# A recurrent attention kernel on one core: the last segment and the drain written as loop passes instead of a tail of their own

## The chip, the cores and the metric

The kernel runs on one core of one Trainium2 chip. A core has a matrix engine (TensorE: PE for matmuls, PEld for its weight loads), VectorE (DVE), ScalarE (ACT), GpSimd (POOL) and a queue that issues transfers (SyncE, SP). The metric is device time in microseconds (us) of one execution. Before the change it is 822.81 us, the median of 3 runs (822.68 to 822.87).

## The reference

The input x has 2048 rows of 512. One branch is an attention over segments of 32 rows with a memory of 8 rows that goes from segment to segment; the other is a layer norm with a two-layer MLP; a gate g of each row mixes both.

```python
mem = mem0
for s in range(64):
    h = concat([mem, x[:, 32 * s:32 * s + 32]])        # 40 rows
    q, k, v = h @ Wq, h @ Wk, h @ Wv                   # 32 heads of 128
    p = softmax(mask(q @ k.T * scale))                 # 40 x 40 for each head
    o = (p @ v) @ Wo
    mem, out_s = o[:8], o[8:]
a = concat(out_0 .. out_63)
b = gelu(layernorm(x) @ w1 + b1) @ w2 + b2
out = g * a + (1 - g) * b
```

The memory that segment 63 leaves is read by nobody.

## The kernel before

The work has two stages. The first, to about 100 us, loads the weights and x and computes the MLP branch and the gates into `c_all` and `g_all`. The second is a loop over the 64 segments (L636), four to a tile of 128 rows; `T, si` are the tile and the segment's place in it. All matmuls of the loop use 32 columns of PE, four products side by side.

A segment handles 32 rows: 8 of memory and 24 of x. The other 8 x rows of each of a tile's four segments ("left" rows) are projected together, as side work of the segments of the tile before (`side_work`, L334). The side work of a tile's fourth segment is `out_units(T - 2)`, which selects the output rows of a tile, adds the MLP branch on DVE (L329) and stores them (L330), and `wo_left(T - 1)`, the output projection of the left rows. These are generators: `run_fill` puts a few of their matmuls where PE would wait. Their results stand in PSUM banks 5 and 6 in turn (`side`, L194); the copies out of them are queued in `dve_q` and `act_q` and are put into the program when `flush` is called.

In order, a segment's pass does this:

- `ux_out(s - 2)` (L630): four ACT copies of the x part of an earlier segment's product into `UTT`, one for each bank.
- `prep_h`, `prep_q`, `x_mul(s - 1)` (L615) on POOL: the x part of the probabilities, `Px`, for the segment before, and the running sum of reciprocals, `racc`.
- Q, K, V (L211, L222), DVE transposes (L217), copies, the scores (L383, L387) on top of a mask that `mask_mm` (L374) wrote into the bank beforehand, and two exponentials on ACT (L685, L686), whose sums go into `hist`.
- The memory half: sums (L688), reciprocal (L692), `Pm` in two parts (L695), the product with V (`av`, L398 and L403), four copies into `UTT` (L703), then the sums and the reciprocal of the x part (L699, L704).
- The output projection (`wo_unit`, L233): 32 matmuls of 512 columns for the memory rows of this segment and the x rows of the segment two before, then a copy to `wsb` (L711).
- The mask of the next segment, the product of `Px` of the segment before with V (`av_x`, L625), and the new memory (L365, L721).

A segment's x rows so reach the output projection two passes later. The pass of segment 63 breaks off after its scores (L683), and a tail of its own follows (L725 to L789): it leaves out the memory half of segment 63; it does the x half on DVE (L733 to L736) instead of POOL; it copies the U banks on DVE and ACT in turn (L755, L763, L765); it runs the projections of segments 61, 62 and 63 (`wo_x`, L744) and that of tile 15's left rows in two halves of 256 columns (L774); and it adds and stores tile 15 in two halves (L788, L789).

The program order of the loop and the tail is kept on each engine (`manual_schedule`, L599 to L790). What stands behind it is placed by the framework where an engine is free: the flag that tells whether any sum overflowed. `hist` is reduced and tested (L796, L799), `racc` likewise (L797, L800), a product with one element counts the partitions that passed (`cnt`, L801 and L802, in one of the two side banks), `bad` follows on DVE (L804), and every engine loads it (L805) and branches on it (L808), past a slow fallback for overflow.

Of the kernel before, what the change touches and what calls it, by code (L numbers as in the profile page):

```python
# [8 lines left out]
FP32 = mybir.dt.float32  # L9
BF16 = mybir.dt.bfloat16  # L10
# [13 lines left out]
def kernel(ctx, tc, A_x, A_mem0, A_Wq, A_Wk, A_Wv, A_Wo, A_seg_len, B_x, B_w1, B_b1, B_w2, B_b2, gate_w, out):  # L24
# [576 lines left out]
    prep_q(0)  # L601
    nc.gpsimd.memset(UTT[1][:, :, :, 0:40], 0.0)
    nc.gpsimd.memset(racc[:], 0.0)
    nc.gpsimd.memset(hist[:], 0.0)
    warm = cw.tile([P, 1], FP32, tag="warm", bufs=1, name="warm")
    nc.scalar.activation(out=warm[:], in_=g_all[:, 0:1], func=ACTF.Exp)
    S_next = mask_mm()
# [25 lines left out]
        for j, U in enumerate(Uxs.pop(s)):  # L633
            nc.scalar.copy(out=UTT[T % 2][:, :, j, c0 + M:c0 + 40], in_=U[:])  # L634

    for s in range(nseg):  # L636
        T, si = divmod(s, SPT)
        last = s == nseg - 1
        hc, hn = hT[s % NHT], hT[(s + 1) % NHT]
        fill = side_work(T, si)  # L640
        if si == 1 and T + 2 < NT:
            x_load(T + 2)
        if si == 3 and T + 1 < NT:
            left_v_in(T + 1)
        if si == 3 and T + 2 < NT:
            x_left(T + 2)
        B, S = S_next
        na, nb, nc_, nd, ne = ring
        ring = (nb, nd, ne, na, nc_)
        qk_banks = (na, nb, nc_, nd, ne)  # L650
        if s >= 2:
            ux_out(s - 2)
            flush(act_q)
        if s + 1 < nseg:
            prep_h(s + 1)
        if s >= 1:
            prep_q(s)
            x_mul(s - 1)
        flush(dve_q)
        BANKS = [(0,) + HF[0], (1,) + HF[0], (0,) + HF[1], (1, H // 2, 3 * H // 4), (1, 3 * H // 4, H)]  # L660
        for bi, (t, h0, h1) in enumerate(BANKS):
            bk = bank(qk_banks[bi], [P, 512])
            for kc in range(KC):
                qk_unit(bk, hc, t, h0, h1, kc)
            Tv = qk_tr(bk, h0, h1)
            dst = QT[:, h0:h1, 0:32] if t == 0 else KT[:, h0:h1, :]
            (nc.gpsimd.tensor_copy if bi == 2 else nc.scalar.copy)(out=dst, in_=Tv)  # L667
        V = cw.tile([P, NG, Dh], BF16, tag="V", name="V")
        Vs[s] = V
        vb0, vb1 = bank(na, [P, 512]), bank(nb, [P, 512])  # L670
        for kc in range(KC):
            v_unit(vb0, hc, 0, kc)
        nc.scalar.copy(out=v_out(V, 0), in_=vb0[:])
        flush(dve_q, 9)
        scores(S, s, 0, 3 * NG // 4)
        v_unit(vb1, hc, 1, 0)
        scores(S, s, 3 * NG // 4, NG)
        for kc in range(1, KC):
            v_unit(vb1, hc, 1, kc)
        E = cw.tile([P, NG, EW], BF16, tag="E", name="E")  # L680
        R = cw.tile([P, NG * 40], FP32, tag="R", name="R")
        Es[s], Rs[s] = E, R
        if last:  # L683
            break
        nc.scalar.activation(out=E[:, :, 0:16], in_=S[:, :, 0:16], func=ACTF.Exp, scale=scale, accum_out=hist[:, s, 0:1])  # L685
        nc.scalar.activation(out=E[:, :, 16:EW], in_=S[:, :, 16:EW], func=ACTF.Exp, scale=scale, accum_out=hist[:, s, 1:2])  # L686
        sm = bank(nc_, [P, NG, 8])
        sums(sm, E[:, :, 8:16], True, False)  # L688
        sums(sm, E[:, :, 0:8], False, True)
        nc.scalar.copy(out=v_out(V, 1), in_=vb1[:])  # L690
        run_fill(5 + (si == 3))
        nc.vector.reciprocal(out=R[:, 0:8 * NG].rearrange("p (i q) -> p i q", q=8), in_=sm[:])  # L692
        Pm = cw.tile([P, NG, 16], BF16, tag="Pm", bufs=1, name="Pm")
        for c in (8, 0):
            nc.vector.tensor_tensor(out=Pm[:, :, c:c + 8], in0=E[:, :, c:c + 8], in1=R[:, 0:8 * NG].rearrange("p (i q) -> p i q", q=8), op=ALU.mult)  # L695
        Um = [bank(k, [P, NG, 8]) for k in (nd, ne, na, nc_)]
        av(Um, 8, s, V, Pm, 8, 0, 0)
        sr = B[:, 0:NG * 32].rearrange("p (i q) -> p i q", q=32)
        sums(sr, E[:, :, 16:48], True, False)  # L699
        sums(sr[:, :, 24:32], E[:, :, 48:56], False, True)  # L700
        Tp, sp = divmod(s - 2, SPT)
        for j in range(4):
            (nc.scalar.copy if j % 2 else nc.vector.tensor_copy)(out=UTT[Tp % 2][:, :, j, 24 - 8 * sp:24 - 8 * sp + M], in_=Um[j][:])  # L703
        nc.vector.reciprocal(out=R[:, 8 * NG:].rearrange("p (i q) -> p i q", q=32), in_=sr)  # L704
        run_fill(1)
        flush(act_q, 2)
        wsb = cw.tile([P, Dm], BF16, tag="wsb", bufs=9, name="wsb")
        wp = bank(nb, [P, Dm])
        for u in range(8):
            wo_unit(wp, UTT[Tp % 2], 24 - 8 * sp, u)  # L710
        nc.scalar.copy(out=wsb[:], in_=wp[:])  # L711
        if s >= 2:
            wsbs[s] = wsb
        S_next = mask_mm()
        if s >= 1:
            av_x(s - 1, (nd, ne, na, nc_))
        run_fill(2 * (si == 3))
        if s + 1 < nseg:
            aT = S_next[0][:, NG * EW:NG * EW + KC * M].rearrange("p (k m) -> p k m", m=M)
            mem_out(aT, wsb)  # L720
            nc.vector.tensor_copy(out=hn[:, :, 0:M], in_=aT)  # L721
        for _ in fill:
            pass

    nc.scalar.activation(out=E[:, :, 16:EW], in_=S[:, :, 16:EW], func=ACTF.Exp, scale=scale, accum_out=hist[:, s, 1:2])  # L725
    nc.scalar.copy(out=v_out(V, 1), in_=vb1[:])
    av_x(s - 1, (nd, ne, na, nc_))
    sr = B[:, 0:NG * 32].rearrange("p (i q) -> p i q", q=32)
    sums(sr, E[:, :, 16:48], True, False)
    sums(sr[:, :, 24:32], E[:, :, 48:56], False, True)  # L730
    Rl = R[:, 8 * NG:]
    Rq = Rl.rearrange("p (i q) -> p i q", q=32)
    nc.vector.reciprocal(out=Rq, in_=sr)  # L733
    Px = cw.tile([P, NG, 40], BF16, tag="Px", name="Px")
    nc.vector.tensor_tensor(out=Px[:, :, 0:32], in0=E[:, :, 16:48], in1=Rq, op=ALU.mult)
    nc.vector.tensor_tensor(out=Px[:, :, 32:40], in0=E[:, :, 48:56], in1=Rq[:, :, 24:32], op=ALU.mult)  # L736
    nc.gpsimd.tensor_tensor(out=racc[:, 8 * NG:], in0=racc[:, 8 * NG:], in1=Rl, op=ALU.add)
    Es.pop(s), Rs.pop(s)
    Pxs[s] = Px
    for _ in fill:  # L740
        pass
    flush(act_q, 9)

    def wo_x(sw, k, ut, c0):  # L744
        wp = bank(k, [P, Dm])
        for u in range(8):
            wo_unit(wp, ut, c0, u)
        wsb = cw.tile([P, Dm], BF16, tag="wsb", bufs=9, name="wsb")
        nc.scalar.copy(out=wsb[:], in_=wp[:])
        wsbs[sw + 2] = wsb  # L750

    U1, U0 = UTT[(NT - 1) % 2], UTT[NT % 2]
    wo_x(s - 2, nb, U1, 16)
    for j, U in enumerate(Uxs.pop(s - 1)):
        (nc.vector.tensor_copy if j % 2 else nc.scalar.copy)(out=U1[:, :, j, 8 + M:48], in_=U[:])  # L755
    for _ in out_units(NT - 2):
        flush(dve_q, 9)
    av_x(s, (nd, ne, na, nc_))
    wo_x(s - 1, nb, U1, 8)

    Ul = Uxs.pop(s)
    for j, U in enumerate(Ul):
        (nc.vector.tensor_copy if j % 2 else nc.scalar.copy)(out=U0[:, :, j, M:32], in_=U[:, :, 0:RIDE])  # L763
    for j, U in enumerate(Ul):
        (nc.vector.tensor_copy if j % 2 else nc.scalar.copy)(out=U1[:, :, j, 32:40], in_=U[:, :, RIDE:32])  # L765
    wo_x(s, 6, U0, 0)
    T = NT - 1
    HD2 = Dm // 2
    wL = cw.tile([P, Dm], BF16, tag="wsbL", bufs=1, name="wsbL")
    for half in range(2):  # L770
        d = slice(HD2 * half, HD2 * half + HD2)
        wp = bank((nc_, nd)[half], [P, HD2])
        for u in range(8):
            wo_unit(wp, U1, 32, u, HD2 * half, HD2 * half + HD2)  # L774
        (nc.vector.tensor_copy if half else nc.scalar.copy)(out=wL[:, d], in_=wp[:])
    o_sb = cw.tile([P, Dm], BF16, tag="o", bufs=1, name="o")
    obs = [bank(k, [P, HD2]) for k in (ne, nb)]
    for half in range(2):
        d = slice(HD2 * half, HD2 * half + HD2)
        for si in range(SPT):  # L780
            nc.tensor.matmul(obs[half][32 * si:32 * si + 32, :], lhsT=SelX[:], rhs=wsbs[SPT * T + si + 2][:, d], start=True, stop=False,
                             tile_position=(0, 32 * si))
    for half in range(2):
        d = slice(HD2 * half, HD2 * half + HD2)
        for si in range(SPT):
            nc.tensor.matmul(obs[half][32 * si:32 * si + 32, :], lhsT=SelL[si][:], rhs=wL[:, d], start=False, stop=True,
                             tile_position=(0, 32 * si))
        nc.vector.scalar_tensor_tensor(out=o_sb[:, d], in0=obs[half][:], scalar=g_all[:, T:T + 1], in1=c_all[:, T, d], op0=ALU.mult, op1=ALU.add)  # L788
        nc.sync.dma_start(out2[T * P:(T + 1) * P, d], o_sb[:, d])  # L789
    man.__exit__(None, None, None)  # L790


# [130 lines left out]
```

## Time and profile before

| | us |
|---|---|
| median of 3 runs | 822.81 (822.68 to 822.87) |
| the profiled execution | 822.87 |
| its span, first to last instruction | 821.1 |
| PE busy | 793.0 (97%) |
| DVE, ACT, POOL busy | 493.1, 446.6, 272.7 |
| granted TensorE clock, mean | 0.998 |

From the trace's table of stretches, with what PE was busy in each:

| stretch, us from the start | length | PE busy |
|---|---|---|
| 785.77 to 796.54 (segment 62) | 10.77 | 9.35 |
| 796.54 to 806.78 (segment 63 and side work) | 10.24 | 10.17 |
| 806.78 to 816.75 (rest of the tail) | 9.97 | 7.12 |
| 816.75 to 821.10 (store, branch, end) | 4.35 | 0.00 |

A line of the timeline has the start, the duration, the engine, the source line, the operation, its tiles and shapes, and in brackets how long the engine idled before and who ended that. A line of the chain has the start, the duration, the engine and the source line of one link of the work that ended last. A line on one source line of the kernel has the engine, the operation, how often it ran, its shortest, median and longest duration in ns, and its first and last start.

### The profile page before, as it was taken

The page shows a single profiled execution, that of the slowest core. Times are in us where ns is not written, and L with a number is a line of the kernel's source. Part 1 is how long each engine was busy: PE and PEld are TensorE (multiplying, and loading weights), DVE is VectorE, ACT ScalarE, POOL GpSimd, SP SyncE. Part 2 cuts the span into 40 slices and gives each one's busy share as a digit, 9 for nine tenths or more (in the row PEclk, how much of TensorE's full clock was granted, in tenths as well). Part 3 has the DMA queues.
Part 4 walks back from the last instruction along what each step waited for, and adds up shares of the span by engine and source line. Part 5 has one row for each costly group of instructions (what it writes and reads, how often), then busy time and mean ns, then how long its engine had stood idle before and what let it go on. Part 6 is the DMA issues. An engine that isn't in the chain of part 4 may idle for free.

```text
span 821.1 us, 48437 instructions
## 1 busy us (share of the span) xinstructions
PE 793.0 (97%) x22013; PEld 443.4 (54%) x22013; DVE 493.1 (60%) x1022; ACT 446.6 (54%) x1239; POOL 272.7 (33%) x624
## 2 busy tenths in 40 slices
PE   6999999999999999999999999999999999999986
PEld 3666545555555555555555555555555555555543
DVE  5764256565656666665666565666566565756554
ACT  3555445655555555555555645555565555565553
POOL 8100224242434243243424242423333242424220
PEclk9999999999999999999999999999999999999999
DMA  9791310000000010101010100101010101010000
GB/s 314 238 404 48 104 28 11 25 16 15 25 20 26 10 36 10 37 11 33 6 38 10 31 17 20 27 18 28 10 36 11 36 4 40 7 34 8 10 5 24
DMA packets 38357, 37.59 MB, mean 46 GB/s; under 512 B 13561, under 2 KB 36578, under 8 KB 36610
## 3 DMA queue, kind: packets, MB, share of 16 engines
q1 hardware_dynamic: 38018, 34.31, 12.6%
q8 instruction: 174, 2.85, 1.5%
q14 instruction: 37, 0.30, 0.1%
q0 software_dynamic: 128, 0.13, 0.1%
HBM read 26.03 MB, written 6.29 MB: 39 GB/s over the span
## 4 chain that ended last, share of the span: by engine, by line
PE 92%; DVE 4%; issue 1%; DMA 1%; SPq 1%; ACT 1%; DVEq 0%; ACTq 0%
PE b L211 33%; PE b L233 18%; PE b L222 16%; PE b L398 5%; PE hp L470 4%; PE bp L487 4%; PE b L360 3%; PE b L374 2%; PE b L365 2%; PE b L383 2%; PE b L403 1%; DVE R L692 1%; DMA Wo_sb<-in_A_x_dram 1%; DVE Pm L695 1%; PE b L387 0%
## 5 line engine op out<-in xcount | busy, mean ns | idle before, releaser
L217 DVE STREAM_TRANSPOSE Tt<-b 128x512 f32<-128x512 f32 (+1 forms) x384 | 225.6, 613 | 82.2 <-PE b L211 70.3
L211 PEld LDWEIGHTS <-hT 128*32 128x32 bf16 x5120 | 131.3, 97 | 108.2 <-DVE hT L721 23.5
L233 PE MATMUL b<-Wo_sb,UTT 128*32 128x512 bf16 (+1 forms) x2656 | 160.9, 378 | 1.3 <-ACT UTT L763 0.9
L222 PE MATMUL b<-Wv_sb,hT 128*32 128x512 bf16 x2048 | 141.8, 378 | 0.0
L211 PE MATMUL b<-Wq_sb,hT 128*32 128x512 bf16 x2048 | 133.3, 380 | 3.2 <-DVE hT L721 1.7
L211 PE MATMUL b<-Wk_sb,hT 128*32 128x256 bf16 (+1 forms) x3072 | 133.3, 308 | 0.0
L667 ACT CAST KT<-Tt 128x256 bf16<-128x256 f32 (+1 forms) x192 | 87.1, 476 | 53.6 <-DVE Tt L217 53.5
L620 POOL TENSOR_TENSOR Px<-E,R 128x256 bf16<-128x256 bf16 x63 | 42.5, 675 | 208.9 <-DVE R L704 208.9
L704 DVE RECIPROCAL R<-b 128x256 f32<-128x256 f32 x63 | 110.7, 1757 | 0.0
L667 POOL CAST QT<-Tt 128x512 bf16<-128x512 f32 x64 | 39.2, 613 | 187.1 <-DVE Tt L217 187.1
L233 PEld LDWEIGHTS <-UTT 128*32 128x32 bf16 x2656 | 64.4, 96 | 63.8 <-DVE UTT L703 12.2
L711 ACT CAST wsb<-b 128x512 bf16<-128x512 f32 x63 | 36.9, 586 | 111.2 <-PE b L233 111.2
L692 DVE RECIPROCAL R<-b 128x64 f32<-128x64 f32 x63 | 35.1, 557 | 78.4 <-PE b L360 78.4
L634 ACT CAST UTT<-b 128x256 bf16<-128x256 f32 x248 | 74.4, 386 | 9.7 <-PE b L403 7.5
L667 ACT CAST QT<-Tt 128x512 bf16<-128x512 f32 x64 | 39.6, 619 | 68.7 <-DVE Tt L217 68.7
L222 PEld LDWEIGHTS <-hT 128*32 128x32 bf16 x2048 | 49.4, 96 | 21.2
L475 ACT ACTIVATE hg<-hp,b_sb 128x256 bf16<-128x256 f32 x80 | 37.8, 474 | 39.9 <-PE hp L470 39.9
L721 DVE CAST hT<-b 128x32 bf16<-128x32 f32 x63 | 12.1, 191 | 79.0 <-PE b L365 79.0
L398 PEld LDWEIGHTS <-V 32*128 32x128 bf16 x4064 | 34.4, 91 | 45.6 <-DVE Pm L695 32.3
L470 PE MATMUL hp<-yT,w_sb 128*128 128x256 bf16 (+1 forms) x352 | 54.7, 281 | 2.2 <-DMA w_sb<-in_B_w_dram 0.9
L703 ACT CAST UTT<-b 128x64 bf16<-128x64 f32 x126 | 20.6, 215 | 66.1 <-PE b L403 66.1
L622 POOL TENSOR_TENSOR racc<-racc,R 128x320 f32<-128x320 f32 x63 | 54.9, 871 | 0.0
(131 smaller groups left out, 1056.5 us busy)
## 6 DMA issues: line engine op xcount, KB each, us to landing
Wv_sb<-in_A_Wv_dram SPq DMA_DIRECT2D x4, 1024.0 KB
Wq_sb<-in_A_Wq_dram SPq DMA_DIRECT2D x4, 1024.0 KB
Wk_sb<-in_A_Wk_dram SPq DMA_DIRECT2D x4, 1024.0 KB
Wo_sb<-in_A_Wo_dram SPq DMA_DIRECT2D x2, 2048.0 KB
vd<-vt SPq DMA_DIRECT2D x32, 128.0 KB
vs<-vd SPq DMA_DIRECT2D x256, 16.0 KB
out_dram<-o SPq DMA_DIRECT2D x15, 128.0 KB
Wo_sb<-in_A_x_dram SPq DMA_DIRECT2D x1, 1024.0 KB
```

What stands on the lines that cost most here:

```text
L211: nc.tensor.matmul(bk[32 * j:32 * j + 32, 0:n], lhsT=G[:, kc, :], rhs=W5[t][:, kc, h0:h1, j, :], start=(kc == 0), stop=(kc == KC - 1), til ...
L217: nc.vector.transpose(out=Tt[:, 0:n], in_=bk[:, 0:n])
L222: nc.tensor.matmul(bk[32 * j:32 * j + 32, :], lhsT=G[:, kc, :], rhs=Wv5[:, kc, 4 * vb:4 * vb + 4, j, :], start=(kc == 0), stop=(kc == KC - ...
L233: nc.tensor.matmul(bk[32 * g:32 * g + 32, :], lhsT=ut[:, i, j, c0:c0 + 32], rhs=Wo_sb[:, 4 * i + j, d0:d1], start=(j == 0 and i < 4), stop ...
L398: nc.tensor.matmul(U[j][:, i, :], lhsT=V[q, i, :], rhs=Pt[q, i, c_main:c_main + n], start=(i == 0), stop=False, skip_group_check=True, til ...
L470: nc.tensor.matmul(hp[:rows, :], lhsT=w1_sb[:, kc, fc * P:fc * P + rows], rhs=yTs[blk][:, kc, :], start=(kc == 0), stop=(kc == KC - 1))
L620: nc.gpsimd.tensor_tensor(out=Px[:, :, 0:32], in0=E[:, :, 16:48], in1=Rr, op=ALU.mult)
L622: nc.gpsimd.tensor_tensor(out=racc[:], in0=racc[:], in1=R[:], op=ALU.add)
L634: nc.scalar.copy(out=UTT[T % 2][:, :, j, c0 + M:c0 + 40], in_=U[:])
L667: (nc.gpsimd.tensor_copy if bi == 2 else nc.scalar.copy)(out=dst, in_=Tv)
L692: nc.vector.reciprocal(out=R[:, 0:8 * NG].rearrange("p (i q) -> p i q", q=8), in_=sm[:])
L704: nc.vector.reciprocal(out=R[:, 8 * NG:].rearrange("p (i q) -> p i q", q=32), in_=sr)
```

## The change

The tail of its own goes. The loop runs over `nseg + 2` passes. Pass 63 is a full pass, with the memory half, whose result is not read. Passes 64 and 65 only drain: `ux_out`, `x_mul` and `av_x` for what is left, and a whole projection each. The rest of tile 14 and tile 15 follow behind the loop with the same generators that the loop uses, each in one piece of 512 columns. The memset of `hist` (L604) goes too, since all of `hist` is now written. The matmuls' tiling, the sums, `Pm` and everything in passes 0 to 62 stay as they are (much of the diff is indentation).

```diff
-    nc.gpsimd.memset(hist[:], 0.0)
...
-    for s in range(nseg):
+    for s in range(nseg + 2):
         T, si = divmod(s, SPT)
-        last = s == nseg - 1
+        live = s < nseg
         hc, hn = hT[s % NHT], hT[(s + 1) % NHT]
-        fill = side_work(T, si)
+        if live:
+            fill = side_work(T, si)
...
-        if last:
-            break
...
+        else:
+            if s == nseg:
+                ux_out(s - 2)
+                x_mul(s - 1)
+                av_x(s - 1, (nd, ne, na, nc_))
+            else:
+                ux_out(s - 2)
+            flush(dve_q)
+            Tp, sp = divmod(s - 2, SPT)
         wsb = cw.tile([P, Dm], BF16, tag="wsb", bufs=9, name="wsb")
         wp = bank(nb, [P, Dm])
         for u in range(8):
...
-        S_next = mask_mm()
-        if s >= 1:
+        if s + 1 < nseg:
+            S_next = mask_mm()
+        if live and s >= 1:
             av_x(s - 1, (nd, ne, na, nc_))
...
-    nc.scalar.activation(out=E[:, :, 16:EW], in_=S[:, :, 16:EW], func=ACTF.Exp, scale=scale, accum_out=hist[:, s, 1:2])
...
-    nc.vector.reciprocal(out=Rq, in_=sr)
...
-    wo_x(s - 2, nb, U1, 16)
-    for j, U in enumerate(Uxs.pop(s - 1)):
-        (nc.vector.tensor_copy if j % 2 else nc.scalar.copy)(out=U1[:, :, j, 8 + M:48], in_=U[:])
-    for _ in out_units(NT - 2):
-        flush(dve_q, 9)
-    av_x(s, (nd, ne, na, nc_))
-    wo_x(s - 1, nb, U1, 8)
...
-    wo_x(s, 6, U0, 0)
...
-            wo_unit(wp, U1, 32, u, HD2 * half, HD2 * half + HD2)
...
-        nc.vector.scalar_tensor_tensor(out=o_sb[:, d], in0=obs[half][:], scalar=g_all[:, T:T + 1], in1=c_all[:, T, d], op0=ALU.mult, op1=ALU.add)
-        nc.sync.dma_start(out2[T * P:(T + 1) * P, d], o_sb[:, d])
+    flush(act_q, 9)
+    for _ in out_units(NT - 2):
+        flush(dve_q, 9)
+    for _ in wo_left(NT - 1):
+        pass
+    flush(act_q, 9)
+    for _ in out_units(NT - 1):
+        pass
+    flush(dve_q, 9)
     man.__exit__(None, None, None)
```

## The prediction

> **What bounds the kernel now.** I read the page's first and fourth parts first: TensorE (PE) is busy 97% of the span and holds 92% of the chain that ended last.
>
> ```profile
> span 821.1 us, 48437 instructions
> PE 793.0 (97%) x22013; PEld 443.4 (54%) x22013; DVE 493.1 (60%) x1022; ACT 446.6 (54%) x1239; POOL 272.7 (33%) x624
> PE 92%; DVE 4%; issue 1%; DMA 1%; SPq 1%; ACT 1%; DVEq 0%; ACTq 0%
> ```
>
> Then I read the diff against the rows. Column tiles of 32, the sums, Pm in two parts (L695 runs twice in each segment) and the projection with 512 columns are all in the trace of before. The loop for segments 0 to 62 is the same text, indented. What differs is the end: segment 63 and all behind it. So the question is the last 25 us, and there PE waits for others. The timeline of before's end:
>
> ```profile
> 806.54 0.17 PE L802 MATMUL b<-good 128*1 128x1 bf16 x1
> 806.76 0.59 ACT L749 CAST wsb<-b 128x512 bf16<-128x512 f32 x1 [1.14 <-PE b L233]
> 807.25 0.65 ACT L755 CAST UTT<-b 128x256 bf16<-128x256 f32 x2
> 807.77 0.14 DVE L804 TENSOR_SCALAR bad<-b 1x1 int32<-1x1 f32 x1
> ...
> 811.28 0.55 ACT L763 CAST UTT<-b 128x192 bf16<-128x192 f32 x2
> 811.65 3.38 PEld L233 LDWEIGHTS <-UTT 128*32 128x32 bf16 x96 [1.41 <-ACT UTT L763]
> ...
> 815.91 0.29 PE L786 MATMUL b<-wsbL,SelL 128*32 128x256 bf16 x4 [0.27 <-DVE wsbL L775]
> ```
>
> Three things are to be seen. The overflow flag (L802, L804) is known at 807.91, far ahead of the end. A copy of ACT starts 0.49 us after the one before it (806.76 to 807.25). And the projection starts 0.04 us after the first of its four UTT copies (811.28 plus 0.33 a copy, to 811.65), not after all four. Last I read what follows the last matmul, by the lines of the branch and of the register load:
>
> ```profile
> L808 ACTq COMPARE_BRANCH  x1: 50/50/50, 815.0 to 815.0; - x1
> L808 PEldq COMPARE_BRANCH  x1: 3429/3429/3429, 816.5 to 816.5; - x1
> L808 DVEq COMPARE_BRANCH  x1: 76/76/76, 816.9 to 816.9; - x1
> ...
> L805 PEldq TENSOR_LOAD <-bad x1: 485/485/485, 815.9 to 815.9; - x1
> ```
>
> PE loads the flag at 815.92 (0.49), branches at 816.51, and that branch takes 3.43 us where the other engines need 0.05 to 0.08. It ends at 819.94; the last record of the span ends at 821.05, 1.11 later. The last store is issued at 816.76 and its wait on SP ends at 819.61, so both end together. **PE's branch sets the end, not the matmuls.**
>
> **The change part by part.** The template for segment 63 as it will run is segment 59, also the fourth of its tile and with the same side work. Its chain:
>
> ```profile
> 759.89 0.29 PE b L398 x32
> 760.18 0.08 PE b L403 x8
> 760.26 0.25 PE b L360 x8
> 760.51 2.00 PE b L233 x36
> 762.52 0.30 PE b L374 x4
> 762.82 0.30 PE b L398 x32
> 763.13 0.08 PE b L403 x8
> ```
>
> The last twelve V matmuls (L222) start at 757.64 there and at 801.37 in segment 63: shift 43.73.
>
> *Segment 63 with its memory half.* The first projection and the side work ahead of it end at 762.52 + 43.73 = 806.25. The mask (L374, 0.30) is not made for a segment 64, so the matmuls of Px follow at once and end at 806.64; the last twelve matmuls of wo_left(14) at 0.054 each give 807.29. Before had done the same products, without the memory half, by 806.78 (end of its chain piece of 64 projection matmuls). So the added sums and Pm matmuls cost 0.5. Its DVE and ACT work (reciprocal 0.56, Pm twice 0.24, four copies of 0.22) is hidden by side work exactly as in segment 59, whose chain has no wait. One thing may break that cover: the reduction of hist and its test (L796, 0.28; L799, 0.16) stand outside the hand-ordered part, and in before they went onto DVE ahead of L733. Ahead of the first reciprocal they would push it from 802.37 to 803.0 and the Pm matmuls by 0.33. I take 0 and keep 0.33 for the range.
>
> *First drain pass (s = 64).* ACT copies wsb at 806.30 and then the four U banks of segment 62 (in segment 59: 1.20 us for four) from 806.80 to 808.00. The same four banks receive segment 63's product, so PE waits from 807.29 for the last bank, 808.04, and ends it 0.36 later, 808.40. Px itself is ready at 807.15 (POOL, 763.42 + 43.73). The projection follows; from its start to its wsb copy the rows have 1.96 (793.35 to 795.31), so that copy starts at 810.36. A rule of the Trainium skill speaks against this part: "TensorEngine Tiling (Array Packing)", under PSUM Bottleneck, wants both ScalarE and VectorE for emptying PSUM, as before did (L755, two copies on each). The trace agrees for this first pass only: two and two would end some 0.5 earlier; in the second pass only the first copy counts, and the rule's gain there is nothing.
>
> *Second pass (s = 65).* ACT is in order: the next U copies start 0.49 behind the wsb copy, at 810.85; the first ends 0.39 later, and PE starts at 811.28 after a stall of about 1 us. The wsb copy of this projection comes at 813.24. Only then does ACT reach the wsbL copy of tile 14, since act_q is emptied after the loop: 813.73 to 814.32. The second half of out_units(14) waits for it: PE at 814.36, a second stall of about 1 us, and wo_left(15) starts 0.21 later, 814.57.
>
> *The last tile in one piece.* Copy to wsbL 1.96 after that start: 816.53 to 817.12; the last four matmuls start at 817.16 (before: 815.91, so **PE ends 1.25 later**). The addition on DVE starts 0.34 behind such matmuls of 256 columns (815.91 to 816.25); I add 0.11, the difference between a matmul of 512 columns (0.39) and of 256 (0.28): 817.61, plus 0.75 (L329) is 818.36.
>
> *The flag.* Its one-element product takes its bank from the same alternating pair as the side work. In before it shared a bank with wo_left(14). Now two more side calls, wo_left(15) and out_units(15), stand ahead of it, so it shares one with wo_left(15) and can't start before that bank is copied out, 817.12. PE then has the last four matmuls first, and DVE has the addition first: bad is ready at 818.36 + 0.14 + 0.01 = 818.51. PE loads it (818.53, 0.49, then 0.10 to the branch): branch at 819.12, plus 3.43 is 822.55, plus 1.11 is 823.66. The store is issued at 818.39. From its issue to a freed buffer the rows have at most 1.84 (L329: 807.88 to 809.72) for 128 KB and 2.85 for before's last half (816.76 to 819.61), so it lands by 821.24, and with the 1.44 from 819.61 to 821.05 would end the span at 822.68 at the latest: hidden behind the branch.
>
> *Dropped memset of hist* (L604, 0.21 on POOL at 102.3): POOL then waits 1.62 us for DVE ahead of L667 anyway; worth 0.
>
> **Sum.** 0.5 in segment 63; about 0.75 net of drain stalls and larger pieces (1.25 in all at the last matmuls); 1.36 because the flag now comes behind the addition. End of span 823.66 against 821.05: +2.61. The profiled execution took 822.87 (span 821.1 and about 1.8 around it), 0.06 over the median of 822.81. So 822.87 + 2.61 = 825.48; I say **825.5**.
>
> The branch is where the skill and the row differ most. "Advanced Engine Details and Errata", under Control Flow Timing, gives about 108 ns for a compare-and-branch; "Runtime: NRT & Kernel Launch", under Instruction fetch mechanics, says that a branch out of the fetched window must wait for a fetch. PE's 3.43 us is against the first and fits the second. By 108 ns the end would be the store's, within 1.6 us of before. The row decides.
>
> **Rivals.**
> *A, the flag comes early.* The framework places L796 to L805 where an engine is free, as it did in before. If bad is ready by 817.16 (another bank, or ahead of the last addition), PE branches at 817.75: end 822.29, and the store's 821.5 to 822.7 counts too. +1.24 to +1.63: 824.1 to 824.5. Against it: the shared bank.
> *B, the flag gets its bank between tile 14 and wo_left(15).* Then PE's 32 matmuls wait until DVE has done the addition of tile 14 and bad: SelL 814.36, addition 814.81 to 815.56, bad 815.70, a delay of 1.15, but the branch is free of the flag: 822.29 + 1.15 = 823.44, or by the store up to 823.8. 825.2 to 825.6, the forecast by another road.
> *C, not slower: PE's branch is short.* All of the forecast beyond the matmuls hangs on 3.43 us at L808 on PE, seen once. If it is no longer than on the other engines, the store ends the span: 821.5 to 822.7, that is 823.3 to 824.5, within 0.2% of before. It decides from a branch under 2.46 us (819.12 + 2.46 + 1.11 = 821.05 + 1.64). For it: four engines branch in under 0.08. Against it: PE is the engine with 44,000 instructions, and neither the branch nor what lies behind it is edited.
> *D, worse.* The 0.33 of hist and a branch or store that is delayed as before's last store was (2.85 against 1.84, so about 1 more) add up to 826.8.
> That the change does nothing: not possible for the order of the end, and true for everything before it.
>
> **How the numbers follow.** The forecast has 0.58 (its own range 825.1 to 825.9), B 0.10, A 0.15, C 0.08, D 0.09. 0.2% of 822.81 is 1.65 us, about what a measurement of this kernel can tell from no change; it lies at 824.46, at A's upper edge. Slower: forecast, B, D and a third of A, 0.82. Same: the rest of A and nearly all of C, 0.17. Faster by that much: 0.01. The range goes from A's lower end, 824.1, to D's 826.8 and leaves out C's lower half and what is beyond D.
>
> **What would show it.** Right: identical rows up to 801; PE's copy-bound waits ahead of segment 63's Px product (0.75), the last full projection (1) and the second half of out_units(14) (1); the last matmuls 1.25 later than 815.91; L802's and L804's counterparts behind the last addition; a PE branch of about 3.4 us. Wrong: a flag ready before the last matmuls (A), a flag in the middle of PE's queue (B), a short branch (C), or any difference within the loop, which I price at nothing.

## The result and the profile after

| | before | after |
|---|---|---|
| median of 4 runs, us | 822.74 (822.18 to 822.87) | 825.71 (825.32 to 825.78) |
| ratio, with 95% interval | 1 | 1.0036 [1.0019, 1.0054] |
| the profiled execution | 822.87 | 825.78 |
| its span | 821.1 | 824.0 |

The change is slower by about 3 us. The page of after, its span, its engines and the shares of its chain:

```profile
span 824.0 us, 48457 instructions
PE 792.8 (96%) x22021; PEld 442.6 (54%) x22021; DVE 490.7 (60%) x1017; ACT 447.9 (54%) x1245; POOL 272.8 (33%) x625
PE 93%; DVE 3%; ACT 1%; DMA 1%; issue 1%; SPq 1%; DVEq 0%; ACTq 0%
```

PE is busy for as long as before (792.8 against 793.0) in a span 2.9 longer: the added time is waiting. The timeline of after's end shows where:

```profile
802.38 0.29 DVE L748 TENSOR_REDUCE tot<-hist 128x1 f32<-128x128 f32 x1 [1.73 <-ACT E L685]
...
802.59 0.55 DVE L691 RECIPROCAL R<-b 128x64 f32<-128x64 f32 x1
...
807.23 0.25 PEld L398 LDWEIGHTS <-V 32*128 32x128 bf16 x3 [0.42 <-ACT UTT L633]
...
811.18 1.91 PE L233 MATMUL b<-Wo_sb,UTT 128*32 128x512 bf16 x32 [0.96 <-ACT UTT L633]
...
814.27 0.40 PE L324 MATMUL b<-wsbL,SelL 128*32 128x512 bf16 x4 [0.96 <-ACT wsbL L311]
...
817.13 0.40 PE L324 MATMUL b<-wsbL,SelL 128*32 128x512 bf16 x4 [0.52 <-ACT wsbL L311]
...
817.35 0.16 PE L754 MATMUL b<-good 128*1 128x1 bf16 x1
817.58 0.75 DVE L329 SCALAR_TENSOR_TENSOR o<-b,g_all,c_all 128x512 bf16<-128x512 f32 x1 [2.12 <-PE b L324]
818.25 0.14 DVE L756 TENSOR_SCALAR bad<-b 1x1 int32<-1x1 f32 x1
```

PE waits for ACT at the last product of `Px`, at the last whole projection, at the second half of `out_units(14)`, and at the last four matmuls. The flag's product (L754) stands behind those, and its result on DVE (L756) behind the last addition. The branch, by its line, and what SP waited for at the end (in all, times, longest):

```profile
L760 PEldq COMPARE_BRANCH  x1: 3829/3829/3829, 819.0 to 819.0; - x1
L760 DVEq COMPARE_BRANCH  x1: 76/76/76, 819.0 to 819.0; - x1
```

```profile
SPq L870 <- PEq L760: 2.4, 1, 2.4
```

SP's long wait at the end is for PE's branch, not for the store, which landed at 820.05. The branch ends at 822.84 and the span at 823.96.

To set kernels beside each other I count from a mark: the start of segment 63's last twelve V matmuls (L222), 801.37 in before and 801.27 in after. Up to there the program is the same but for a memset, and after runs ahead of before by 0.09 to 0.83 on the way; that it is 0.10 at the mark is chance. In us from the mark ("last matmuls" is the start of the last four):

| kernel | last matmuls | flag ready | PE's branch starts | lasts | last store issued | landed | end of span |
|---|---|---|---|---|---|---|---|
| before | 14.54 | 6.53 | 15.13 | 3.43 | 15.39 | 18.22 | 19.68 |
| after | 15.86 | 17.12 | 17.74 | 3.83 | 17.09 | 18.78 | 22.69 |

So the profiled 2.91 us (825.78 - 822.87) are: 1.32 at the last matmuls; 1.29 because the flag comes behind them; 0.40 in the branch itself; -0.10 ahead of the mark, which is chance: in the thirteen profiles of the two tables the mark stands anywhere from 800.84 to 802.14.

### The profile page after: what moved, and what is told of

It reads as the page before. It is cut to its first block, busy times and chain, and to the rows that moved or that the text cites. A ratio compares the mean times of both kernels' runs of the same rounds, so it can differ in the third digit from the quotient of the medians.

```text
span 824.0 us, 48457 instructions
## 1 busy us (share of the span) xinstructions
PE 792.8 (96%) x22021; PEld 442.6 (54%) x22021; DVE 490.7 (60%) x1017; ACT 447.9 (54%) x1245; POOL 272.8 (33%) x625
## 4 chain that ended last, share of the span: by engine, by line
PE 93%; DVE 3%; ACT 1%; DMA 1%; issue 1%; SPq 1%; DVEq 0%; ACTq 0%
PE b L211 34%; PE b L233 18%; PE b L222 16%; PE b L398 5%; PE hp L470 4%; PE bp L487 4%; PE b L360 3%; PE b L374 2%; PE b L365 2%; PE b L383 2%; PE b L403 1%; DMA Wo_sb<-in_A_x_dram 1%; PE b L387 0%; PE b L324 0%; DVE hT L730 0%
## 5 line engine op out<-in xcount | busy, mean ns | idle before, releaser
L233 PE MATMUL b<-Wo_sb,UTT 128*32 128x512 bf16 x2624 | 161.5, 380 | 1.3 <-ACT UTT L633 1.0
L222 PE MATMUL b<-Wv_sb,hT 128*32 128x512 bf16 x2048 | 141.8, 378 | 0.0
L703 DVE RECIPROCAL R<-b 128x256 f32<-128x256 f32 x64 | 112.4, 1757 | 0.0
L719 ACT CAST wsb<-b 128x512 bf16<-128x512 f32 x66 | 38.6, 585 | 116.6 <-PE b L233 116.6
L633 ACT CAST UTT<-b 128x256 bf16<-128x256 f32 x256 | 76.8, 387 | 9.9 <-PE b L403 8.0
L222 PEld LDWEIGHTS <-hT 128*32 128x32 bf16 x2048 | 49.4, 96 | 21.2
```

Source lines behind the costliest of these rows:

```text
L222: nc.tensor.matmul(bk[32 * j:32 * j + 32, :], lhsT=G[:, kc, :], rhs=Wv5[:, kc, 4 * vb:4 * vb + 4, j, :], start=(kc == 0), stop=(kc == KC - ...
L233: nc.tensor.matmul(bk[32 * g:32 * g + 32, :], lhsT=ut[:, i, j, c0:c0 + 32], rhs=Wo_sb[:, 4 * i + j, d0:d1], start=(j == 0 and i < 4), stop ...
```

## Experiments

The theory was the prediction's: three waits in a row on the path of one chain (drain, flag, PE's branch). The main rivals were that the branch does not bind (the store does), and that the cost sits in one place alone. Each ratio is against the kernel before on the same chip, with its 95% interval, of 11 runs or so (6 for the first split); before's median was 822.86, 823.36 or 823.17 there. The ratio is made from all runs, not from the two medians. The interval of after itself (1.0019 to 1.0054) overlaps those of its single repairs, so what one repair is worth is read from the profiles, by the times from the mark.

| kernel | median, us | ratio | last matmuls | branch starts | lasts | store issued | landed | end |
|---|---|---|---|---|---|---|---|---|
| after, flag early | 824.29 | 1.0017 [1.0008, 1.0025] | 15.86 | 16.45 | 3.50 | 17.08 | 19.73 | 21.06 |
| after, no fallback | 823.18 | 1.0005 [0.9996, 1.0014] | 15.86 | 17.74 | 0.23 | 17.09 | 18.77 | 20.16 |
| before, no fallback | 821.35 | 0.9979 [0.997, 0.9988] | 14.54 | 15.13 | 0.24 | 15.63 | 17.20 | 18.40 |
| before, flag late | 823.55 | 1.0011 [1.0003, 1.002] | 14.55 | 16.11 | 3.78 | 15.40 | 16.94 | 21.00 |
| after, wsbL early | 824.17 | 1.0018 [1.0009, 1.0027] | 14.72 | 16.61 | 3.44 | 15.95 | 17.64 | 21.16 |
| after, no memory half in 63 | 825.0 | 1.0021 [1.0013, 1.003] | 15.17 | 17.05 | 3.59 | 16.39 | 18.09 | 21.76 |
| after, split copies | 827.24 | 1.0051 [1.0037, 1.0066] | 18.56 | 20.45 | 3.43 | 19.79 | 21.48 | 24.99 |
| after, split and flag early | 824.31 | 1.0016 [1.0007, 1.0025] | 15.43 | 16.03 | 3.71 | 16.66 | 19.53 | 20.86 |
| before, one segment per pass in the fallback | 823.36 | 1.0002 [0.9993, 1.0011] | 14.54 | 15.14 | 3.54 | 15.39 | 18.33 | 19.81 |
| before, looped fallback | 821.43 | 0.9981 [0.9972, 0.999] | 14.54 | 15.13 | 0.64 | 15.39 | 18.50 | 19.76 |
| after, all together | 822.94 | 0.9997 [0.9988, 1.0006] | 14.03 | 14.63 | 0.38 | 15.26 | 18.35 | 19.68 |

### The flag

In after, the flag's code by hand in pass 64, its product in a bank that is free:

```diff
         nc.scalar.copy(out=wsb[:], in_=wp[:])
+        if s == nseg:
+            okp = loop.enter_context(tc.tile_pool(name="okp", bufs=1))
...
+            cnt = bank(7, [1, 1])
+            nc.tensor.matmul(cnt[:], lhsT=good[:, 0:1], rhs=good[:, 1:2], start=True, stop=True)
...
-    cnt = side([1, 1])
```

> The changed kernel with its flag early: the reductions, the product with one element (in bank 7, which is free by then) and bad are written by hand into pass 64. Theory (PE's branch sets the end and in the changed kernel waits for the flag behind the last addition): PE loads the flag at 817.14 instead of 818.42, all before stays, the span ends 1.28 earlier, 822.7, and the time is 824.4. Rival 1 (the last store sets the end): no difference, 825.7. Rival 2 (the whole loss is in the drain's stalls, the flag costs nothing): no difference, 825.7.

The flag was ready at 9.17 instead of 17.12, PE branched 1.29 earlier, and the time fell to 824.29. The last matmuls did not move. (The end came 1.63 earlier, because the branch also lasted 0.33 less.) The branch's end (19.95) and the store's landing (19.73) now lie 0.2 apart, so further gains need both.

The same thing the other way round, in before: the reductions ahead of the projection of segment 63, `cnt` and `bad` behind the last addition.

```diff
+    okp = loop.enter_context(tc.tile_pool(name="okp", bufs=1))
...
     wo_x(s, 6, U0, 0)
...
         nc.sync.dma_start(out2[T * P:(T + 1) * P, d], o_sb[:, d])
+    cnt = side([1, 1])
+    nc.tensor.matmul(cnt[:], lhsT=good[:, 0:1], rhs=good[:, 1:2], start=True, stop=True)
...
     man.__exit__(None, None, None)
```

> The kernel before with its flag late: the product with one element and bad stand by hand behind the last matmuls and the last addition; the two reductions stand where DVE is idle, ahead of the projection of segment 63. Theory (PE's branch sets the end): bad is ready at 816.88 instead of 807.91, PE branches at 817.48 instead of 816.51, span 822.0, time 823.7. Rival 1 (the store sets the end): 822.7. Rival 2 (the early flag had cost PE a wait of 1.19 in the middle of the tail, so taking it away gives back as much as the late flag costs): 822.5 to 822.7.

PE branched at 16.11 instead of 15.13 after the mark, 0.97 later, with the last matmuls and the store's issue where they were. The end moved by 1.32, because the branch also lasted 0.35 longer. The ratio says 0.9 us (0.25 to 1.65). Rival 2 falls: PE waits 1.19 at the same place (L320) as before, now for DVE's addition. The two runs together show the flag's place as a cause on its own, worth 1.29 in after and 0.97 in before, where the last addition is of half the columns.

### The branch

The fallback left out, but for its first transfer and transposes, in both kernels:

```diff
             mem_tr()
-            mk = gp.tile([L, L], FP32)
...
-                nc.sync.dma_start(out2[bass.ds(Ti * P, P), :], og[:])
```

> The changed kernel with nearly all of the overflow fallback left out (a branch over a few instructions stays; these inputs never enter it). Theory (PE's branch takes 3.8 us because its target lies behind some 3,700 instructions of PE): the branch takes about 0.05 to 0.1, and the end is set by the last store, which landed at 820.05, plus the 1.44 that before needed from its store to the end: span about 821.5, time 823.3. Rival (the 3.8 us are a wait for something else, such as a fetch that is due anyway): span 824.0, time 825.7.

> The kernel before with nearly all of the overflow fallback left out. Theory (branch and store end together there): the branch goes to under 0.1, and the store alone sets the end: between 820.0 (if it then lands 1.7 after its issue, as other stores do) and 821.1; time 821.7 to 822.7. Rival (the 3.4 us of the branch are a wait for something else): 822.7 with a branch of 3.4.

After's branch in that kernel, by its line:

```profile
L760 PEldq COMPARE_BRANCH  x1: 228/228/228, 819.0 to 819.0; - x1
```

The branch has the same condition and flag at the same place; only the code it jumps over is gone, and 3.83 us become 0.23. The other engines take 0.05 to 0.08 in before and after alike. With the branch short the store ends both kernels, and after is still 1.83 slower than before (823.18 against 821.35): rival C of the prediction describes what is left, but its condition, a short branch, does not hold in the real kernel.

How much code is too much? PE has some 3,660 instructions in the fallback, counting each matmul and its weight load. With one segment for each pass of its loop, results through a buffer in HBM, it has 930:

```diff
-            with tc.For_i(0, NT) as Ti:
-                nc.sync.dma_start(x_sb[:], x2[bass.ds(Ti * P, P), :])
...
-                for si in range(SPT):
+            with tc.For_i(0, nseg) as Si:
+                nc.sync.dma_start(x_sb[:], x2[bass.ds(Si * seg, seg), :])
```

> The kernel before with the same overflow fallback written shorter: one segment for each pass of its loop instead of four, its rows through a buffer in HBM, so that PE's branch passes some 930 instructions instead of some 3,660. Theory (the branch's time comes from the distance of its target): if 930 are near enough, a branch of 0.1 to 0.3, span 819.6 to 820.0, time 821.4; if they are still too far, a branch of 3.4 and 822.7, and then the distance at which it decides is shorter. Rival (what counted in the run without the fallback was something else that left with it): 822.7.

```profile
L808 PEldq COMPARE_BRANCH  x1: 3539/3539/3539, 816.8 to 816.8; - x1
```

No change: 930 are still too many. With an inner loop as well, four heads in each pass, it has some 140:

```diff
+            HC = 4
...
+            with tc.For_i(0, nseg) as Si:
...
+                with tc.For_i(0, H // HC) as Hi:
+                    for t, W in enumerate((Wq_sb, Wk_sb, Wv_sb)):
+                        nc.vector.tensor_copy(out=ws[:, t], in_=W[:, :, bass.ds(Hi * (HC * Dh), HC * Dh)])
...
+                    nc.vector.tensor_tensor(out=ao[:], in0=ao[:], in1=xo[:], op=ALU.add)
```

> The kernel before; the fallback behind the branch computes the same in loops: one segment for each pass of an outer loop, four heads for each pass of an inner one, so that PE has some 140 instructions in the branch instead of 3,660 (and 930 in the kernel with one segment for each pass, where the branch still took 3.54 us). Theory, the time of PE's branch is a fetch of instructions that lie too far ahead, and it has a threshold under 930: with 140 it takes 0.2 to 0.3 us, as with the fallback left out (0.24), the last store lands 1.6 to 1.7 us after its issue instead of 2.8, and the kernel takes 821.2 to 821.8 beside 822.8 for before. Rival, any branch over code that is not already fetched costs PE the whole fetch, however short: 3.4 to 3.8 us at the branch and 822.7 to 823.4, no change. Nothing ahead of the branch differs in either.

```profile
L808 PEldq COMPARE_BRANCH  x1: 642/642/642, 817.3 to 817.3; - x1
```

0.64 instead of 3.43, and a ratio of 0.9981: this kernel is faster than before by 1.6 us (0.8 to 2.3), and so than after, and it leaves nothing out. Its profiled execution took 823.66, far over its median of 821.43, so its row in the table is no picture of the usual end: 0.77 of that lies ahead of the mark, and its store landed 3.1 after its issue. What its price is when the fallback is needed:

> The kernel before with the looped fallback of 140 PE instructions, and the test at the branch turned round (the fallback runs when no sum overflowed), so that every execution takes it. It tells what the short form of the fallback costs when it is needed, and whether PE's branch is as short when it is not taken. Estimate from rows of before: in one inner pass some 70 PE instructions of 0.01 to 0.1 us, and about 20 instructions of DVE and ACT in one chain, four of them copies of weights (2048 columns of bf16), at 0.2 to 2 us each, so 8 to 25 us; 512 inner passes give 4 to 13 ms, against the 0.82 ms of the main path. Theory, the branch that falls through to the next instruction needs no far fetch: 0.05 to 0.3 us at the branch on PE. Rival, PE's branch empties what was fetched in either direction: 0.6 us or more there.

```profile
L808 PEldq COMPARE_BRANCH  x1: 95/95/95, 816.4 to 816.4; - x1
```

An execution that takes the fallback needs 8349 us, inside the estimate. Here the branch falls through to the next instruction, where all other kernels jump over the fallback, and it costs PE 0.095. So PE's branch time is set by where its target lies.

The records of single transfer packets say what the long branch waits for. In all nine profiles with 930 or more PE instructions behind the branch, a 16 KB packet of instructions starts 1.04 to 1.18 us after the branch does and takes 0.96 to 1.34, and the branch ends 1.34 to 1.38 after the packet. Before has 1.10 + 0.96 + 1.37 = 3.43, after 1.18 + 1.31 + 1.34 = 3.83: the packet alone makes 0.35 of the 0.40 between them. Without the fallback no such packet follows the branch. With the looped fallback one starts 1.37 us after the branch (1.10 in the last kernel below), when the branch is already over. The records do not say which engine a packet is for; the reading rests on the times.

One rule of the Trainium skill fits these rows and another does not. "Runtime: NRT & Kernel Launch", under Instruction fetch mechanics, says that a taken branch (one that jumps) beyond the fetched window waits for a fetch. "Advanced Engine Details and Errata", under Control Flow Timing, has about 108 ns for a compare-and-branch. On PE the runs show nearly that (0.095 us) only where the branch does not jump.

### The drain and the memory half

In after, the copy of tile 14's left rows (`wsbL`) is emptied from `act_q` in pass 64 instead of behind the loop:

```diff
                 av_x(s - 1, (nd, ne, na, nc_))
+                flush(act_q, 9)
```

> The changed kernel with one line more: the copy of tile 14's left rows to wsbL is put into pass 64, behind the U copies, instead of behind the loop. Theory (the second stall of PE, 0.96 ahead of the second half of out_units(14), reaches the end in full): that wait goes, everything behind it comes about 1.0 earlier, the branch too; span 823.0, time 824.7. Rival (the gain is lost again: the copy pushes the wsb or U copies on ACT, or the end is held by the store): 825.4 to 825.7.

```profile
807.32 0.64 ACT L311 CAST wsbL<-b 128x512 bf16<-128x512 f32 x1
...
812.70 0.39 PE L324 MATMUL b<-wsbL,SelL 128*32 128x512 bf16 x4
...
815.56 0.40 PE L324 MATMUL b<-wsbL,SelL 128*32 128x512 bf16 x4 [0.53 <-ACT wsbL L311]
```

The copy stands at 807.32 instead of 813.62, the first of the two L324 groups has no wait in brackets, and the last matmuls come 1.14 earlier. One line takes back nearly all of the 1.32.

After without the memory half of segment 63 (its sums, `Pm`, product and copies), as before had it:

```diff
-            nc.vector.reciprocal(out=R[:, 0:8 * NG].rearrange("p (i q) -> p i q", q=8), in_=sm[:])
+            if mem:
+                nc.vector.reciprocal(out=R[:, 0:8 * NG].rearrange("p (i q) -> p i q", q=8), in_=sm[:])
...
```

> The changed kernel without the memory half of segment 63 (its sums, reciprocal, Pm, product with V and copies; nobody reads their result). Theory (the 8 sums and 40 Pm matmuls lie on PE's path, their DVE and ACT work beside it): 0.5 less, span 823.5, time 825.2. Rival (side work had covered a wait for Pm that is not seen in the chain, or the matmuls filled a wait): 0.9 less or nothing, 824.8 or 825.7.

The last matmuls came 0.69 earlier. That is the price of work whose result is read by nobody. The remaining 0.63 of the 1.32 is the drain's net cost: before's tail has waits of its own, so that the early `wsbL` alone could win more than that.

### Two engines for the U copies

In after, the four `UTT` copies of each drain pass on ACT and DVE in turn:

```diff
-            nc.scalar.copy(out=UTT[T % 2][:, :, j, c0 + M:c0 + 40], in_=U[:])
+            (nc.vector.tensor_copy if drain and j % 2 else nc.scalar.copy)(out=UTT[T % 2][:, :, j, c0 + M:c0 + 40], in_=U[:])
```

> The changed kernel with the U copies of passes 64 and 65 on ACT and DVE in turn, as the tail of before had them. Theory (the first pass's product waits for the last of four copies, the second pass's projection only for the first, which stays on ACT): 0.4 to 0.5 less, all of it ahead of the product of Px; span 823.5, time 825.2. Rival 1 (both passes gain): 0.9 to 1.0 less, 824.7. Rival 2 (copies on two engines out of PSUM slow each other, or DVE's addition comes later and holds a bank): nothing, 825.7.

It was slower, by 2.70 at the last matmuls of the profiled execution, which took 828.58, 1.34 over the median of the six. My expectation fell. The timeline says why:

```profile
808.40 0.49 DVE L749 TENSOR_REDUCE tot<-racc 128x1 f32<-128x320 f32 x1 [1.94 <-POOL racc L621]
808.92 0.16 DVE L752 TENSOR_SCALAR good<-tot 128x1 bf16<-128x1 f32 x1
809.00 0.76 DVE L633 CAST UTT<-b 128x256 bf16<-128x256 f32 x2
809.48 0.68 PE L398 MATMUL b<-Px,V 32*128 32x32 bf16 x31 [1.57 <-DVE UTT L633]
...
810.17 3.25 PE L233 MATMUL b<-Wo_sb,UTT 128*32 128x512 bf16 x32
```

The framework had put the flag's reduction of `racc` onto DVE ahead of the new copies. It waits 1.94 for POOL, the copies start behind it and its test (809.00), and PE waits 1.57 for them. Then a second loss: the next 32 matmuls take 3.25 where they took 1.91. The table of stretches (length, busy PE, PEld, DVE, ACT, POOL, then PE's granted clock) has the clock beside it:

```profile
806.90:808.50 1.60, 1.00 (x29) 0.35 (x18) 0.10 (x1) 0.93 (x3) 1.47 (x3) 1.00 0.04 10
808.50:810.10 1.60, 0.48 (x39) 0.38 (x38) 1.57 (x5) 0.00 (x0) 0.00 (x0) 1.00 0.00 0
810.10:812.00 1.90, 1.90 (x43) 0.88 (x32) 0.57 (x2) 0.00 (x0) 0.00 (x0) 0.63 0.19 69
812.00:813.60 1.60, 1.41 (x16) 0.25 (x8) 0.32 (x2) 0.15 (x1) 0.00 (x0) 0.50 0.00 0
```

Behind 3.2 us with PE busy for 1.48, the last 1.6 of them for 0.48, the granted clock has a mean of 0.63 and then 0.50. After kept 1.00 through a stretch with PE busy for half of it:

```profile
810.10:812.00 1.90, 0.94 (x20) 0.44 (x20) 0.00 (x0) 1.69 (x5) 0.00 (x0) 1.00 0.00 0
```

How much idle time it takes, no run here shows. The 1.34 that the slow matmuls cost (3.25 - 1.91) is also what this execution took over the median, so the usual run may have the first loss alone. The run had two losses in it, so the split was tried again with the flag's code placed by hand behind the copies of pass 64:

> The kernel after with the flag's code by hand in pass 64 (as in the kernel with the early flag, 824.29, its last matmuls 15.86 us after the mark of segment 63), and the U copies of both drain passes on ACT and DVE in turn. The same split without the flag moved took 827.24. Theory, the split itself is good and it was the flag's reductions, put onto DVE ahead of the copies, that cost the time: here they stand behind the copies of pass 64, the four copies end 0.3 to 0.5 earlier, and the last matmuls come at 15.3 to 15.6; 823.8 to 824.1. Rival, the copies on DVE are the trouble whatever stands ahead of them (slower, or behind DVE's other work): last matmuls at 16.3 or later, 824.8 to 826.5.

```profile
807.01 0.76 DVE L633 CAST UTT<-b 128x256 bf16<-128x256 f32 x2 [0.68 <-PE b L403]
...
807.52 0.54 PEld L398 LDWEIGHTS <-V 32*128 32x128 bf16 x32 [0.42 <-ACT UTT L633]
...
808.34 0.28 DVE L723 TENSOR_REDUCE tot<-hist 128x1 f32<-128x128 f32 x1
...
811.04 1.91 PE L233 MATMUL b<-Wo_sb,UTT 128*32 128x512 bf16 x32 [0.96 <-ACT UTT L633]
```

Now the copies go first, and the last matmuls come at 15.43, 0.43 before those of the kernel with the early flag alone (0.5 was said of two and two). So the queue's order, not the split, had cost the time. All of the gain is in the first pass; the second still waits 0.96 for its first copy. The Trainium skill, "TensorEngine Tiling (Array Packing)", under PSUM Bottleneck, asks for both engines to empty PSUM. The prediction had given this rule 0.5 in the first pass and nothing in the second, and the two rows agree. The kernel's time did not follow: 1.0016 against 1.0017, inside the intervals. In the two profiles the branch lasted 0.21 longer here, and the store landed only 0.20 earlier.

### All together

After with the early flag, the early `wsbL`, no memory half in 63, and the looped fallback.

> The kernel after with four edits at once: the flag by hand in pass 64, the wsbL copy of tile 14 emptied ahead of pass 65, no memory half in segment 63 (its result is read by nobody), and the fallback in loops with some 140 PE instructions. One by one the edits moved the last matmuls by 0, -1.14 and -0.69 us from 15.86 after the mark. Theory, the waits lie one behind the other and add up: last matmuls at 14.0 (before has 14.54). If the short fallback makes the branch short (0.24), the last store sets the end, 18.0 to 18.2 after the mark, and the kernel takes 820.9 to 821.3, below before and after; if the branch stays at 3.5, 822.2 to 822.6. Rival, the edits share a wait: last matmuls at 14.4 to 14.7, and each time 0.4 to 0.7 more.

The waits add up: the last matmuls came at 14.03, as forecast, 0.51 ahead of before, and the branch lasted 0.38. The time did not follow: 822.94 where 820.9 to 821.3 was forecast, no different from before. The store was issued at 15.26 and landed 3.09 later instead of 1.7. The records of single packets, sorted from five traces (us from the start of the span), show what held it:

```
kernel                     16 KB instruction packet   last store packet       first store packet
                           start     end              ahead of a gap, start   behind it, start
before                     817.61    818.57           817.92                  818.55
after, flag early          818.86    819.94           819.73                  819.92
after, split, flag early   818.67    819.93           819.52                  819.92
before, looped fallback    818.64    819.71           818.68                  819.70
after, all together        817.36    818.79           818.19                  818.78
```

Each time most of the store's packets pass, and the last 8 to 16 start just as a 16 KB packet of instructions ends. Before with one segment per pass shows the same (end 819.01, first packet behind 818.99). In after that packet starts at 820.20, behind the store, which lands 1.7 after its issue. So a transfer of instructions delays the last store when the two meet, by some 1 to 1.5 us. This reading rests on times that agree in six traces; the records do not name the DMA engine.

It is the same packet that follows PE's branch, 1.04 to 1.37 us behind the branch's start. In the six kernels with a late store the branch starts ahead of the store's issue (here 14.63 against 15.26); in the five others that have the packet it starts behind it. So a flag that comes early enough also brings this packet onto the last store. Why the looped fallback gains 1.6 us in before and the combined kernel nothing stays open: the end is the store's in both profiles, and no execution of the first near its median was profiled. An estimate from the rows: its profiled 823.66 less the 0.77 ahead of the mark, and with a store that lands after 1.56 us as in before without the fallback, not 3.11, would be 821.3, near the median of 821.43.

## Why the prediction was right, step by step

- **The place.** The loop to segment 62 was priced at nothing. At the mark the traces are 0.10 apart, and on the way up to 0.83; this is the wandering of one execution against another and no cost of the change, and that it ended so small is luck.
- **Segment 63's memory half.** Put at 0.5; taking it out gave 0.69. The reductions of `hist` did go ahead of the reciprocal (802.38 against 802.59), as feared, but the `Pm` product started at 803.45, 803.55 with the 0.10 ahead of the mark, and segment 59's template says 803.62: worth 0, as taken.
- **The drain.** Put at 0.75 net; 0.63 is what the memory half leaves of 1.32. The two terms were off by 0.19 and 0.12 in opposite directions, so their sum of 1.25 is nearer to 1.32 than either is to its own row. Each wait stood where it was foreseen: stalls of 0.96 and 0.96 for "about 1" and "about 1". The first, put at 0.75, shows as PE taking the banks one by one as they come free: 32 products of `Px` take 1.06 where those of segment 62 took 0.37. They and the eight behind them end at 808.37; 808.40 was said.
- **The flag.** Put at 1.36; it measured 1.29 by the start of the branch, and moving it alone gave 1.29 in after and, the other way, 0.97 in before. The flag's product stood behind the last four matmuls (817.35 against 817.13), which rules out rivals A and B; whether the shared bank held it there or its place in the program was not tested.
- **The branch.** Taken as 3.43 from the one row of before; in after it was 3.83. This is the term that was mis-sized, by 0.40. In nine profiles with 930 or more PE instructions behind the branch it lasted 3.43 to 3.83, so one row could not give it closer than that; the spread goes with the packet of instructions that the branch waits for (0.96 to 1.34).
- **The store.** Said to be hidden, and it was: SP waited 2.4 for PE's branch. Rival C's short branch would have left after within 0.2% of before, and the kernel without the fallback is just that (1.0005).

Sum: 2.61 put, 2.91 measured in the profiled executions; the 0.40 of the branch less 0.10 ahead of the mark is the difference. The last matmuls came 0.07 later than put and the flag cost 0.07 less, which cancels by chance.

## What to carry to other kernels

A drain that reuses the loop's body also takes over the loop's queue order: look for copies that the loop's steady state hid (here `wsbL`, one line, 1.14 us) and for code without a fixed place, such as a flag, that now lands last. Where a branch jumps over a fallback that is rarely needed, ask how many instructions each engine jumps over, and see when its flag is ready; both are outside the busy table. Then look whether the branch's transfer of instructions meets the last store. When a repair makes things slower, look at what stands ahead of the moved work in its new queue before giving up the idea.

## What the runs showed of the hardware

- PE's branch over the fallback took 3.43 to 3.83 us with 930 or more PE instructions to jump over, 0.38 to 0.64 with some 140, 0.23 to 0.24 with nearly none, and 0.095 when it did not jump. The long ones end 1.34 to 1.38 us after a 16 KB packet of instructions that starts 1.04 to 1.18 us after the branch.
- In one trace the granted clock of PE fell to a mean of 0.63 and then 0.50 behind 3.2 us with PE busy for 1.48, and 32 matmuls took 3.25 us instead of 1.91. The Trainium skill, "TensorE: Matmul & The Clock Gate", Part 1, names an idle window of about 3.4 us for such a fall. Here PE was busy for part of that time, by the rows above.
- A last store that met a 16 KB packet of instructions landed 2.65 to 3.11 us after its issue (six traces), and 1.53 to 1.70 otherwise (seven).
